# Half a key tile as VectorE's last softmax work, and turned denominators for the second last unit

## The chip, the core and the metric

The kernel runs on one core of a Trainium2 chip. The metric is the device time of one execution in microseconds. Five engines work from queues of their own: TensorE (PE in the profile; its weight loads are PEld), VectorE (DVE), ScalarE (ACT), GpSimd (POOL) and SyncE (SP); the last two, and ScalarE, also issue DMAs. Each engine takes its instructions in the order in which they were written, and an instruction that has to wait holds up those behind it on its engine.

## The reference

A gate mixes attention and a feed-forward block over the same input x (2048 x 512, bf16). There are 32 heads of 16 columns each.

```python
qkv = (x @ wqkv)...                              # q, k, v: 32 heads of 2048 x 16
scores = jnp.einsum("bhqd,bhkd->bhqk", q, k) * (Dh ** -0.5)
p = softmax(scores, axis=-1)
o = jnp.einsum("bhqk,bhkd->bhqd", p, v)
a = o.transpose(...).reshape(B, S, D) @ wo
b = (silu(x @ w_gate) * (x @ w_up)) @ w_down
g = sigmoid((x * gate_w).sum(-1, keepdims=True))
out = g * a + (1 - g) * b
```

## The kernel before

**Units and key tiles.** The queries form 4 blocks of 512 and the heads 8 groups of 4. One block of queries with one group of heads is a unit (`UNIT`, L115), so there are 32 units, 0 to 31. A unit has 16 key tiles of 128 keys. A key tile has four score blocks, one for each head, of 128 keys by 512 queries. TensorE computes a score block, an engine takes its exponential, and TensorE multiplies the result with v and adds it up over the unit's 16 key tiles in the accumulator `o_ps` (`pv`, L882). v has a column of ones, so that the softmax denominators come out as rows 0, 32, 64 and 96 of the accumulator, beside 16 rows of output for each head.

**Two engines share the exponentials.** ScalarE takes two score blocks at a time (`emit_pair`, L731): TensorE writes a tile `s_t` of 128x1024 in PSUM, of which there are two buffers, and one ACTIVATE makes `e_t` of it. VectorE takes whole key tiles from the end of a unit (`emit_d`, L764): each of the four score blocks comes in a PSUM bank of its own (`d_t`, three banks shared with all other small work, `m_tile`) and is scaled and converted to an integer in `y_t`, which is an approximate exponential by its bits. Then come five wide steps over the 128x2048 of the key tile that correct it: z is masked out of y, u is a linear function of z, u is squared, u is multiplied by z, u is added to y, and a last step (`last`, called its close below) shifts and scales y. The add is mostly a DMA that accumulates, issued from GpSimd; for the last work of unit 31 it is an instruction of VectorE (`here_add`, L791).

**The order.** The program keeps a plan of the times of TensorE, VectorE and ScalarE with costs written in the code, and places each instruction by it, before anything runs. `v_unit` (L1386) decides whether VectorE takes a further key tile: only if its work queued so far and a lead (`LEAD` 16.0 us, and `LAST` 8.5 us for unit 31) end before ScalarE would reach that tile. `next_pv` and the loops behind L1419 put the products with v, the feed-forward block and the projections into the time that TensorE has left beside the scores.

**The end of a unit.** The accumulator is evicted to `osb` (`post`). For most units the denominators go through DRAM to be inverted. The last two units take no such way. For unit 30 (`last_recip`, L1251) one matmul with `sbc_t` copies each denominator to the 32 rows of its head in PSUM (`dl`, 128x512), and VectorE inverts this in four quarters of 128x128, each followed by its product with `osb`. For unit 31 the code behind the loops (from L1500) does otherwise: four small matmuls with the columns of `osb` as weights and `sel_t` as the moving operand put the denominators into a tile of 128x16 (`dt`), with queries on the partitions; VectorE inverts these 16 columns (`rt`); sixteen matmuls with the identity as the moving operand turn and spread them again over 128x512 (`rps`); and the product with `osb` follows. The output projection of the last block of queries adds up in `a_l_a`, `a_l_b`, `al` and `al_o`.

Of the kernel before, what the change touches and what calls it, by code (L numbers as in the profile page):

```python
# [9 lines left out]
ALU = mybir.AluOpType  # L10
AX = mybir.AxisListType
BF16 = mybir.dt.bfloat16
F32 = mybir.dt.float32
U16 = mybir.dt.uint16
# [65 lines left out]
def kernel(  # L80
# [13 lines left out]
    P = 128  # L94
    x = A_x.flatten_outer_dims()
    S, D = x.shape
    F = B_w_gate.shape[1]
# [59 lines left out]
    def mm(*args, **kw):  # L157
        return ordered(nc.tensor.matmul(*args, **kw))  # L158
# [143 lines left out]
    def spend(mode, mms, ready=0.0):  # L302

        plan.seq += 1
        work_at.append((plan.pe, mms))
        plan.pe = max(plan.pe + (0.1 if mode != plan.mode else 0.0), ready) + (0.226 if mode == "F" else 0.216) * mms
        plan.mode = mode

    def later(cost, f, ready=None, key=None):

        c = plan.chain
        if c is not None:
            c.owed += 1
        ready = plan.pe + 0.25 if ready is None else ready
        owed.insert(sum(o[0] <= ready for o in owed), (ready, cost, f, c, key))
# [32 lines left out]
    def m_tile(name):  # L348
        while m_ready() is None:
            stuck()  # L350
        i = min((i for i in range(3) if banks[i] is not None), key=lambda i: banks[i])
        plan.pe = max(plan.pe, banks[i])
        banks[i] = None
        held[i] = ps_m[i].tile([P, QBW], F32, tag=f"m{i}", name=name)
        return held[i]

    def m_free(ps, t):
        i = [h is ps for h in held].index(True)
        banks[i], held[i] = t + 0.2, None
# [352 lines left out]
    pv_turn = [True]  # L712
    vready = []
    vcur = {}

    HEADS = (0, 2, 1, 3)

# [45 lines left out]

    def emit_d():  # L764
        if not vcur:
            vcur.update(n=v_take(), i=0, y=vex.tile([P, NV * QBW], U16, tag="y", name="y_t", bufs=NY))
            y_live[0] += 1
        n, i, y = vcur["n"], vcur["i"], vcur["y"]
        vcur["i"] += 1
        d_t = m_tile("d_t")  # L770
        score(d_t[:, :], 4 * n + i)
        spend("R", 1)
        e_of[4 * n + i] = y[:, i * QBW:(i + 1) * QBW].bitcast(BF16)
        if i == NV - 1:
            vcur.clear()

        def first():
            vec.tensor_scalar(out=y[:, i * QBW:(i + 1) * QBW], in0=d_t[:, :], scalar1=EXP_A, scalar2=EXP_B,
                              op0=ALU.mult, op1=ALU.add)
            m_free(d_t, plan.dve)  # L780
            if i < NV - 1:
                return
            z = vex.tile([P, NV * QBW], U16, tag="z", name="z_t")
            u_turn[0] ^= 1
            if u_turn[0]:

                ua = (kaug[:, 0, :] if au > QB else wd_t[:, 0:4, :].rearrange("p f d -> p (f d)")).bitcast(F16)
            else:
                ua = vex.tile([P, NV * QBW], F16, tag="u", name="u_t")[:, :]
            ya, za = y[:, :], z[:, :]  # L790
            here_add = n >= SLOTS - KT and act_end() - plan.dve < 4.2 + ADD_US  # L791
            key = ("y", n)
            plan.last = key
            vops.extend([
                (0.6, lambda: vec.tensor_scalar(out=za, in0=ya, scalar1=0x1FF, scalar2=0x800, op0=ALU.bitwise_and,
                                                 op1=ALU.bitwise_or), key, n),
                (0.6, lambda: vec.tensor_scalar(out=ua, in0=za, scalar1=EXP_K, scalar2=EXP_M, op0=ALU.mult,
                                                 op1=ALU.add), key, n),
                (1.135, lambda: vec.tensor_tensor(out=ua, in0=ua, in1=ua, op=ALU.mult), key, n),
            ])  # L800

            def add_here():
                vec.tensor_tensor(out=ya, in0=ya, in1=ua, op=ALU.add)
                added.append((plan.dve, last, n))

            def add():
                vec.tensor_tensor(out=ua, in0=ua, in1=za, op=ALU.mult)
                if here_add:
                    vops.append((1.135, add_here, None, n))
                    return  # L810
                nc.gpsimd.dma_start(out=ya, in_=ua, accum_op=ALU.add)  # L811
                added.append((plan.dve + ADD_US, last, n))

            def last():
                vec.tensor_scalar(out=ya, in0=ya, scalar1=EXP_D, scalar2=0.25, op0=ALU.add, op1=ALU.mult)
                vready.append((plan.dve + 0.4, n))
            vops.append((1.135, add, None, n))
        d_wait.append((plan.pe + 0.25, first, n))

    def pay_d():  # L820
# [119 lines left out]
    def recip16(o, i):  # L940
        with nc.allow_low_precision(reason="bf16 reciprocal of softmax denominators is plenty accurate here"):
            vec.reciprocal(o, i)
# [27 lines left out]
                normed.add((qb, b))  # L970
            at.setdefault(n0 + 13 + b, []).append(lambda norm=norm: later(0.345, norm))

    def recip_here(osb):

        dps = m_tile("dl")
        mm(dps[:, :], lhsT=sbc_t[:, :], rhs=osb[:, :], start=True, stop=True)
        rd = work.tile([P, QBW], BF16, tag="rd", name="rd")
        return dps, rd

    here_done = []  # L980
    a_ps = []
# [71 lines left out]
    def turn(dc, ps):  # L1053
        for k in range(2 * TQ):
            mm(ps[k // TQ][:, k % TQ * P:(k % TQ + 1) * P], lhsT=x_rows[:, k, (dc - HALF) * P:(dc - HALF + 1) * P],
               rhs=ident[:, :], start=True, stop=True)
# [179 lines left out]
    au = at_ = half = 0  # L1236
    vu = 0
    hi = [KT] * UNITS
    here = {}

    def finish(un):
        settle(un)
# [7 lines left out]

    def last_recip(un):  # L1251

        here[un] = recip_here(osbs[un])
        spend("F", 1)
        for i in range(TQ):
            def part(cs=slice(i * P, (i + 1) * P)):
                recip16(here[un][1][:, cs], here[un][0][:, cs])
                vec.tensor_tensor(out=osbs[un][:, cs], in0=osbs[un][:, cs], in1=here[un][1][:, cs],
                                  op=ALU.mult)
                if cs.stop == QBW:  # L1260
                    m_free(here[un][0], plan.dve)
                    here_done.append(un)
            later(1.2, part)

    def close(un):
        def f():
# [104 lines left out]
        emit_pv(ns[0])  # L1371

    SLACK = 0.1
    LEAD, LAST = 16.0, 8.5
    TILE_US = 1.87

    def forward():
# [3 lines left out]

    def act_end():
        left = [hi[u] - (at_ + half if u == au else 0) for u in range(au, UNITS)]
        return plan.act + sum(left) * TILE_US

    def v_unit():  # L1386

        nonlocal vu
        if y_live[0] >= NY or sum(v[0] for v in vops) > 1.4 or (au, at_) < (0, 2):
            return None  # L1390
        while vu < UNITS:
            if vu > au + 1 or vu in q_of and not (q_of[vu].done() and (vu < QB or plan.slot >= q_of[vu].done_at + 3)):
                return None
            left = hi[vu] - (at_ + half if vu == au else 0)
            if vu >= au and left > 0:
                end = plan.act + (left - 1) * TILE_US + ((hi[au] - at_) * TILE_US if vu > au else 0.0)
                if plan.dve + sum(v[0] for v in vops) + 0.6 * len(owed) + (LEAD if vu < UNITS - 1 else LAST) <= end:
                    return vu
            vu += 1
        return None  # L1400

    def v_take():
        un = v_unit()
        hi[un] -= 1
        n = un * KT + hi[un]
        forward()
        return n

    def want_d():
        if not vcur and v_unit() is None:  # L1410
            return False
        c = pick()
        one = c is not None and c.pieces[c.i][2] and (pace.credit > 0 or c.deadline <= plan.slot + 4)
        if len(d_wait) >= (1 if one else 2):
            return False
        t = m_ready(2 if one and int(c.pieces[c.i][2]) == 1 else 1)
        return t is not None and t <= plan.pe

    while au < UNITS:  # L1419
# [41 lines left out]
        n = au * KT + at_  # L1461
        emit_pair([4 * n + 2 * half, 4 * n + 2 * half + 1])
        half ^= 1
        at_ += not half
        forward()
    flush_act()
# [32 lines left out]
    osb = osbs[un]  # L1499
    tail(2)  # L1500
    dt = m_tile("dt")
    for tq in range(TQ):
        mm(dt[:, 4 * tq:4 * tq + 4], lhsT=osb[:, tq * P:(tq + 1) * P], rhs=sel_t[:, :], start=True, stop=True)
    rt = work.tile([P, 4 * TQ], BF16, tag="rt", name="rt")
    recip16(rt[:, :], dt[:, 0:4 * TQ])
    tail(2)
    rps = ps_s.tile([P, 2 * QBW], F32, tag="s", name="rps")
    for tq in range(TQ):
        for j in range(4):
            mm(rps[32 * j:32 * j + 32, tq * P:(tq + 1) * P],  # L1510
               lhsT=rt[:, 4 * tq + j:4 * tq + j + 1].broadcast_to([P, 32]), rhs=ident[:, :],
               start=True, stop=True, tile_position=(0, 32 * j), skip_group_check=True)
    tail(len(rest))
    on_l = work.tile([P, QBW], BF16, tag="rd", name="on_l")
    for tq in range(TQ):
# [46 lines left out]
```

## Time and profile before

| What | Value |
|---|---|
| Median of four runs | 828.84 us (826.58 to 829.12) |
| Profiled execution, time | 827.2 us |
| Profiled execution, span from the first to the last instruction | 825.5 us |
| Exponentials on ScalarE, e_t<-s_t | 842, 785.0 us busy |
| Score blocks on VectorE, y_t<-d_t | 364, 236.9 us busy |
| Granted clock of TensorE | 1.000 |

The chain that ended last, by the page, is a mixture of ScalarE and TensorE to which no single line contributes more than 6% of the span: the two hand on to each other all the time. Durations in the timelines are from start to end of an instruction; neighbours on one engine overlap a little, so the starts tell the pace. A line of a timeline with a count (x7) merges neighbours of one kind, and its duration goes from the first start to the last end. L158, L161 and L170 are the lines of helpers that record the instructions of TensorE, ScalarE and VectorE, so groups are told apart by their tiles.

### The profile page before, as it was taken

What the parts mean: (1) busy time and instruction counts of PE and PEld (TensorE: products, weight loads), DVE (VectorE), ACT (ScalarE), POOL (GpSimd) and SP (SyncE); (2) the same over time, 40 slices, a digit from 0 to 9 for tenths busy, and PEclk for the clock granted to TensorE, in tenths of its full rate; (3) what the DMA queues carried; (4) which work ended last, traced back from release to release, by engine and by line L of the source; (5) the groups of instructions that cost most, each with busy time, mean ns of one, the idle gap of its engine ahead of it and who ended that gap; (6) DMA issues with size and microseconds to landing.
All of it is one profiled execution on the core that took longest, in us unless ns stands there. A gap on an engine that the chain in (4) does not pass through costs nothing. (4 is left out here: it accounts for less than half of the span.)

```text
span 825.5 us, 20380 instructions
## 1 busy us (share of the span) xinstructions
PE 784.4 (95%) x8109; PEld 231.0 (28%) x8110; DVE 795.6 (96%) x1178; ACT 809.0 (98%) x911; POOL 105.8 (13%) x124
## 2 busy tenths in 40 slices
PE   8999999999999999899999999899999999899996
PEld 3322332322222222222222222222222222222222
DVE  6899999999999999999999999999999999999995
ACT  6999999999999999999999999999999999999996
POOL 5010111110111100101111111001111011111110
PEclk9999999999999999999999999999999999999999
DMA  7044346574543345465434455544344546534432
GB/s 179 12 77 91 57 89 124 123 160 97 109 93 74 77 97 126 93 126 101 84 72 94 104 126 115 112 78 100 74 93 88 117 103 120 106 62 88 85 82 58
DMA packets 101096, 79.75 MB, mean 97 GB/s; under 512 B 75745, under 2 KB 89033, under 8 KB 101001
## 3 DMA queue, kind: packets, MB, share of 16 engines
q0 software_dynamic: 12960, 47.19, 31.0%
q1 hardware_dynamic: 86312, 30.93, 15.8%
q8 instruction: 63, 1.03, 0.5%
q10 hardware_dynamic: 1728, 0.33, 0.2%
q14 instruction: 33, 0.26, 0.1%
HBM read 21.55 MB, written 2.35 MB: 29 GB/s over the span
## 5 line engine op out<-in xcount | busy, mean ns | idle before, releaser
L161 ACT ACTIVATE e_t<-s_t 128x1024 bf16<-128x1024 f32 x842 | 785.0, 1107 | 2.1 <-PE s_t L158 1.5
L158 PE MATMUL s_t<-qx,kaug 64*128 64x512 bf16 x1336 | 274.6, 383 | 25.7 <-ACT e_t L161 22.3
L170 DVE TENSOR_SCALAR y_t<-d_t 128x512 uint16<-128x512 f32 x364 | 236.9, 680 | 2.4 <-PE d_t L158 1.9
L158 PEld LDWEIGHTS <-kaug 64*128 64x128 bf16 x2048 | 110.3, 93 | 338.5 <-issue 328.9
L158 PE MATMUL o_ps<-e_t,vaug 128*32 128x512 bf16 x1684 | 167.9, 390 | 0.0
L158 PE MATMUL d_t<-qx,kaug 64*128 64x512 bf16 x296 | 100.2, 379 | 1.8 <-DVE y_t L170 0.5
L811 POOL DMA_DIRECT2D y_t<-u_t x45 | 46.6, 1036 | 356.1 <-PE s_t L158 228.6
L158 PEld LDWEIGHTS <-vaug 128*32 128x32 bf16 x2052 | 50.0, 93 | 121.4 <-issue 120.4
L811 POOL DMA_DIRECT2D y_t<-kaug x39 | 41.9, 1073 | 281.7 <-PE s_t L158 139.4
L158 PE MATMUL gu<-xT,wg 128*32 128x512 bf16 x896 | 76.1, 383 | 0.9 <-DMA wg<-in_B_w_gate_dram 0.6
L158 PE MATMUL gu<-xT,wu 128*32 128x512 bf16 x896 | 73.8, 382 | 0.0
L170 DVE TENSOR_SCALAR z_t<-y_t 128x2048 uint16<-128x2048 uint16 x91 | 62.4, 685 | 1.0
L170 DVE TENSOR_SCALAR y_t<-y_t 128x2048 uint16<-128x2048 uint16 x91 | 62.0, 683 | 1.3 <-DMA y_t<-u_t 0.8
L158 PE MATMUL ops<-wd_t,mt 128*32 128x512 bf16 x672 | 56.7, 383 | 0.0
L170 DVE TENSOR_TENSOR u_t<-u_t 128x2048 f16<-128x2048 f16 x45 | 54.8, 1218 | 0.8
L170 DVE TENSOR_TENSOR u_t<-u_t,z_t 128x2048 f16<-128x2048 f16 x45 | 54.6, 1214 | 0.1
L170 DVE TENSOR_TENSOR kaug<-kaug 128x2048 f16<-128x2048 f16 x40 | 48.8, 1221 | 1.0
L170 DVE TENSOR_TENSOR kaug<-kaug,z_t 128x2048 f16<-128x2048 f16 x40 | 48.5, 1214 | 0.1
L158 PE MATMUL s_t<-q,kaug 64*128 64x512 bf16 x208 | 42.3, 383 | 2.7 <-ACT e_t L161 2.4
L170 DVE SCALAR_TENSOR_TENSOR mt<-gs,gu 128x512 bf16<-128x512 bf16 x56 | 38.1, 680 | 2.5 <-PE gu L158 0.2
L170 DVE SCALAR_TENSOR_TENSOR gs<-th,gu 128x512 bf16<-128x512 bf16 x56 | 38.0, 679 | 0.3
L161 ACT ACTIVATE th<-gu 128x512 bf16<-128x512 f32 x56 | 37.7, 673 | 0.0
(147 smaller groups left out, 572.9 us busy)
## 6 DMA issues: line engine op xcount, KB each, us to landing
y_t<-u_t POOLq DMA_DIRECT2D x45, 512.0 KB, 5.1
y_t<-kaug POOLq DMA_DIRECT2D x39, 512.0 KB, 5.1
wg<-in_B_w_gate_dram SPq DMA_DIRECT2D x56, 128.0 KB
wu<-in_B_w_up_dram SPq DMA_DIRECT2D x56, 128.0 KB
y_t<-wd_t POOLq DMA_DIRECT2D x6, 512.0 KB, 5.0
on<-osb SPq DMA_DIRECT2D x120, 16.0 KB
rb<-rr SPq DMA_DIRECT2D x15, 128.0 KB
wd_t<-in_B_w_down_dram SPq DMA_DIRECT2D x7, 256.0 KB
```

Source lines behind the costliest of these rows:

```text
L158: return ordered(nc.tensor.matmul(*args, **kw))
L161: ordered(nc.scalar.activation(*args, **kw))
L170: return lambda *a, **kw: ordered(f(*a, **kw))
L811: nc.gpsimd.dma_start(out=ya, in_=ua, accum_op=ALU.add)
```

## The change

Three things are changed.

1. When no whole key tile can be given to VectorE any more, `v_half` may give it two of the four score blocks of one key tile of unit 31, once. ScalarE takes the first two blocks of that tile, as one pair, and VectorE the last two; all its steps are then 1024 columns wide in place of 2048 (`cols`), the add is done on VectorE, and the tile's product with v waits for both halves.
2. The denominators of unit 30 are inverted as those of unit 31: four small matmuls (`denominators`), a reciprocal of 128x16, sixteen matmuls (`spread_rows`) into the same bank, and one product of 128x512. The four steps are placed as two chains of side work, the second released after the first.
3. The lead `LAST` is 10.5 us in place of 8.5, with 6.0 us for the half tile (`LAST_HALF`), and the limit under which the add is done on VectorE is 6.2 us and the add's 6.0 in place of 4.2 and 6.0.

The tail behind the loops is the same code, with its two groups of matmuls moved into the new functions.

```diff
     def emit_d():
         if not vcur:
-            vcur.update(n=v_take(), i=0, y=vex.tile([P, NV * QBW], U16, tag="y", name="y_t", bufs=NY))
+            n, i = v_take()
+            vcur.update(n=n, i=i, y=vex.tile([P, NV * QBW], U16, tag="y", name="y_t", bufs=NY))
...
+        cols = slice(2 * QBW if n in halved else 0, NV * QBW)
+        part = (NV * QBW - cols.start) / (NV * QBW)
...
-            ya, za = y[:, :], z[:, :]
-            here_add = n >= SLOTS - KT and act_end() - plan.dve < 4.2 + ADD_US
+            ya, za, ua = y[:, cols], z[:, cols], ua[:, cols]
+            full, wide = 0.07 + 0.53 * part, 0.07 + 1.065 * part
+            here_add = n >= SLOTS - KT and (n in halved or act_end() - plan.dve < 6.2 + ADD_US)
...
             def last():
                 vec.tensor_scalar(out=ya, in0=ya, scalar1=EXP_D, scalar2=0.25, op0=ALU.add, op1=ALU.mult)
+                if n in halved:
+                    for k in (2, 3):
+                        e_end[4 * n + k] = plan.dve + 0.4
+                    return
                 vready.append((plan.dve + 0.4, n))
...
-    def recip_here(osb):
-
-        dps = m_tile("dl")
-        mm(dps[:, :], lhsT=sbc_t[:, :], rhs=osb[:, :], start=True, stop=True)
-        rd = work.tile([P, QBW], BF16, tag="rd", name="rd")
-        return dps, rd
+    def denominators(p, osb):
+        for tq in range(TQ):
+            mm(p[:, 4 * tq:4 * tq + 4], lhsT=osb[:, tq * P:(tq + 1) * P], rhs=sel_t[:, :], start=True, stop=True)
+
+    def spread_rows(p, rt):
+        for tq in range(TQ):
+            for j in range(4):
+                mm(p[32 * j:32 * j + 32, tq * P:(tq + 1) * P],
+                   lhsT=rt[:, 4 * tq + j:4 * tq + j + 1].broadcast_to([P, 32]), rhs=ident[:, :],
+                   start=True, stop=True, tile_position=(0, 32 * j), skip_group_check=True)
...
     def last_recip(un):
 
-        here[un] = recip_here(osbs[un])
-        spend("F", 1)
-        for i in range(TQ):
-            def part(cs=slice(i * P, (i + 1) * P)):
-                recip16(here[un][1][:, cs], here[un][0][:, cs])
-                vec.tensor_tensor(out=osbs[un][:, cs], in0=osbs[un][:, cs], in1=here[un][1][:, cs],
-                                  op=ALU.mult)
-                if cs.stop == QBW:
-                    m_free(here[un][0], plan.dve)
-                    here_done.append(un)
-            later(1.2, part)
+        st = {}
+        osb = osbs[un]
+
+        def turn():
+            st["p"] = m_tile("dl")
+            denominators(st["p"], osb)
+            spend("F", 1)
+            later(0.3, invert)
+
+        def invert():
+            st["r"] = work.tile([P, 4 * TQ], BF16, tag="rt", name="rt")
+            recip16(st["r"][:, :], st["p"][:, 0:4 * TQ])
+
+        def spread():
+            spread_rows(st["p"], st["r"])
+            spend("F", 2)
+            later(0.67, norm)
+
+        def norm():
+            vec.tensor_tensor(out=osb[:, :], in0=osb[:, :], in1=st["p"][:, :], op=ALU.mult)
+            m_free(st["p"], plan.dve)
+            here_done.append(un)
+        c = pace.add([(1, turn, True, "F", None)], 0, plan.slot + 2)
+        pace.add([(2, spread, False, "F", None)], 0, plan.slot + 4, [c], 1)
...
-    LEAD, LAST = 16.0, 8.5
+    LEAD, LAST, LAST_HALF = 16.0, 10.5, 6.0
...
+    def v_half():
+
+        un = UNITS - 1
+        if halved or au < un or y_live[0] >= NY or hi[un] - at_ < 3:
+            return False
+        busy = sum(v[0] for v in vops) + 0.6 * (len(owed) + len(d_wait) + len(added))
+        return plan.dve + busy + LAST > act_end() and plan.dve + busy + LAST_HALF <= act_end() - 0.5 * TILE_US
+
     def v_take():
         un = v_unit()
+        if un is None:
+            halved.append((UNITS - 1) * KT + hi[UNITS - 1] - 1)
+            return halved[0], 2
...
     def want_d():
-        if not vcur and v_unit() is None:
+        if not vcur and v_unit() is None and not v_half():
             return False
```

More of the change, by code (lines that the diff above doesn't have):

```diff
@@ L714 @@
     vcur = {}
+    halved = []
     HEADS = (0, 2, 1, 3)
@@ L794, in first @@
             vops.extend([
-                (0.6, lambda: vec.tensor_scalar(out=za, in0=ya, scalar1=0x1FF, scalar2=0x800, op0=ALU.bitwise_and,
+                (full, lambda: vec.tensor_scalar(out=za, in0=ya, scalar1=0x1FF, scalar2=0x800, op0=ALU.bitwise_and,
                                                  op1=ALU.bitwise_or), key, n),
-                (0.6, lambda: vec.tensor_scalar(out=ua, in0=za, scalar1=EXP_K, scalar2=EXP_M, op0=ALU.mult,
+                (full, lambda: vec.tensor_scalar(out=ua, in0=za, scalar1=EXP_K, scalar2=EXP_M, op0=ALU.mult,
                                                  op1=ALU.add), key, n),
-                (1.135, lambda: vec.tensor_tensor(out=ua, in0=ua, in1=ua, op=ALU.mult), key, n),
+                (wide, lambda: vec.tensor_tensor(out=ua, in0=ua, in1=ua, op=ALU.mult), key, n),
             ])
@@ L808, in add @@
                 if here_add:
-                    vops.append((1.135, add_here, None, n))
+                    vops.append((wide, add_here, None, n))
                     return
@@ L815, in last @@
                 vec.tensor_scalar(out=ya, in0=ya, scalar1=EXP_D, scalar2=0.25, op0=ALU.add, op1=ALU.mult)
+                if n in halved:
+                    for k in (2, 3):
+                        e_end[4 * n + k] = plan.dve + 0.4
+                    return
                 vready.append((plan.dve + 0.4, n))
-            vops.append((1.135, add, None, n))
+            vops.append((wide, add, None, n))
         d_wait.append((plan.pe + 0.25, first, n))
@@ L1238 @@
     hi = [KT] * UNITS
-    here = {}
     def finish(un):
@@ L1383, in act_end @@
         left = [hi[u] - (at_ + half if u == au else 0) for u in range(au, UNITS)]
-        return plan.act + sum(left) * TILE_US
+        return plan.act + (sum(left) - 0.5 * len(halved)) * TILE_US
     def v_unit():
         nonlocal vu
-        if y_live[0] >= NY or sum(v[0] for v in vops) > 1.4 or (au, at_) < (0, 2):
+        if halved or y_live[0] >= NY or sum(v[0] for v in vops) > 1.4 or (au, at_) < (0, 2):
             return None
@@ L1406, in v_take @@
         forward()
-        return n
+        return n, 0
     def want_d():
-        if not vcur and v_unit() is None:
+        if not vcur and v_unit() is None and not v_half():
             return False
@@ L1463 @@
         half ^= 1
+        if n in halved:
+            half = 0
         at_ += not half
@@ L1501 @@
     dt = m_tile("dt")
-    for tq in range(TQ):
-        mm(dt[:, 4 * tq:4 * tq + 4], lhsT=osb[:, tq * P:(tq + 1) * P], rhs=sel_t[:, :], start=True, stop=True)
+    denominators(dt, osb)
     rt = work.tile([P, 4 * TQ], BF16, tag="rt", name="rt")
@@ L1507 @@
     rps = ps_s.tile([P, 2 * QBW], F32, tag="s", name="rps")
[L1508 to L1512, printed above, removed]
+    spread_rows(rps, rt)
     tail(len(rest))
```

## The prediction

> **What bounds the kernel now.** I began with the page's totals. ScalarE is busy in 98% of the span and VectorE in 96%, so nothing can be gained by moving work between them except where one of them stops early, and that is at the end.
>
> ```profile
> span 825.5 us, 20380 instructions
> PE 784.4 (95%) x8109; PEld 231.0 (28%) x8110; DVE 795.6 (96%) x1178; ACT 809.0 (98%) x911; POOL 105.8 (13%) x124
> ```
>
> Next I set the instruction order of the two built programs side by side. It differs from the point where unit 30 (the second last) is normalised; all before that point is the same on every engine. On SP and POOL the order is the same to the end: no DMA is added, dropped or moved past another, the output store of o_t alone comes with its later VectorE instruction. The whole effect must therefore arise after about 797 us, and the timeline of the last 30 us is the view that decides. ScalarE first (start, duration, engine, operation, idle before):
>
> ```profile
> 810.12 6.63 ACT L161 ACTIVATE e_t<-s_t 128x1024 bf16<-128x1024 f32 x7
> 817.58 0.60 ACT L161 ACTIVATE osb<-o_ps 128x512 bf16<-128x512 f32 x1 [0.83 <-PE o_ps L158]
> ```
>
> The seven exponentials end at 816.75 and the last one takes about 1.2 (longer than the group mean of 1.107 on the page), so six starts fill 6.63 - 1.2 = 5.43 us: one exponential every 0.904 us, back to back. The eviction of the last unit (osb) starts 0.83 after them. Now VectorE over the same stretch:
>
> ```profile
> 797.15 0.69 DVE L170 TENSOR_SCALAR u_t<-z_t 128x2048 f16<-128x2048 uint16 x1
> 797.76 0.95 DVE L170 RECIPROCAL rd<-dl 128x128 bf16<-128x128 f32 x1
> 798.74 0.23 DVE L170 TENSOR_TENSOR osb<-osb,rd 128x128 bf16<-128x128 bf16 x1
> 798.89 0.95 DVE L170 RECIPROCAL rd<-dl 128x128 bf16<-128x128 f32 x1
> ...
> 802.27 1.22 DVE L170 TENSOR_TENSOR u_t<-u_t 128x2048 f16<-128x2048 f16 x1
> 803.40 1.28 DVE L170 TENSOR_SCALAR y_t<-d_t 128x512 uint16<-128x512 f32 x2
> ...
> 809.70 1.23 DVE L170 TENSOR_TENSOR kaug<-kaug 128x2048 f16<-128x2048 f16 x1
> 810.97 1.23 DVE L170 TENSOR_TENSOR kaug<-kaug,z_t 128x2048 f16<-128x2048 f16 x1
> 812.22 1.22 DVE L170 TENSOR_TENSOR y_t<-y_t,kaug 128x2048 uint16<-128x2048 uint16 x1
> 813.68 1.30 DVE L170 TENSOR_SCALAR y_t<-y_t 128x2048 uint16<-128x2048 uint16 x2 [0.23 <-DMA y_t<-u_t]
> 818.52 0.26 DVE L170 RECIPROCAL rt<-dt 128x16 bf16<-128x16 f32 x1 [3.54 <-PE dt L158]
> ```
>
> VectorE stops at 814.98 and stands idle for 3.54 us, while ScalarE works until 816.75: this is the slack that can be used. The starts also give a rule for the sums below: an instruction that needs the one before starts 0.04 after its end (798.74 after 797.76 + 0.95), one that doesn't starts 0.08 before it (798.89 after 798.74 + 0.23). TensorE last:
>
> ```profile
> 815.29 0.40 PE L158 MATMUL o_ps<-e_t,vaug 128*32 128x512 bf16 x4
> 815.52 0.39 PE L158 MATMUL o_ps<-y_t,vaug 128*32 128x512 bf16 x4
> 815.84 0.39 PE L158 MATMUL a_l_a<-bblk,ident 64*128 64x512 bf16 x1
> ...
> 816.16 0.82 PE L158 MATMUL al<-wo_t,on 128*128 128x512 bf16 x2
> 816.91 0.40 PE L158 MATMUL o_ps<-y_t,vaug 128*32 128x512 bf16 x4
> 817.14 0.39 PE L158 MATMUL o_ps<-e_t,vaug 128*32 128x512 bf16 x4
> ```
>
> None of these waits for anything: from 815.29 TensorE's own queue leads to the last o_ps at 817.14, 0.4 after the last exponential. So the end is set by ScalarE's pace and then by 1.85 us of queued matmuls. What follows (817.58 to 825.5, 7.92 us) is the same code in both kernels and stays.
>
> **Parts of the change.** *ScalarE.* Half a key tile, one pair of score blocks, goes to VectorE: 841 exponentials in place of 842. At 0.904 a start, the last one ends at 816.75 - 0.90 = 815.85, if it meets no more waits than now.
>
> *VectorE loses* the four reciprocals of 128x128 and their products: 797.76 to 802.27, 4.51 us. *It gains* one reciprocal of 128x16 (the same instruction is the last line above: 0.26), one product 128x512 with a PSUM operand, two evictions of scores (0.60 each by the pair at 803.40), and six half-wide steps. The product has no exact row. From below it is the group on<-on,rb (128x512, SBUF alone, 415 ns), from above the four quarters on_l<-osb,rps with the same kinds of operand (0.88 together); I take 0.68, the mean of the rows of this width that read PSUM. Half-wide steps (128x1024, 16 bit) have none either. TENSOR_SCALAR takes 285 ns at 512 columns (group aq<-qst) and 685 at 2048, so 0.42 in between; TENSOR_TENSOR 415 and about 1220, so 0.68. The bounds are those ends: three of each kind, 1.2 us earlier or 2.4 us later in all.
>
> A rule of the Trainium skill speaks against the half tile: "VectorE: DVE Perf Modes", section on the TRN2 errata, says that each instruction pays a fixed latency once, so that small tiles pay it more often. This case shows it too: the two TENSOR_SCALAR rows lie on a line with 0.15 us at no columns, so six half-steps carry about 0.9 us that buys nothing. By the page's formula (58 cycles and the columns over the mode's factor at 0.96 GHz) they would take an estimated 0.33 and 0.59, and the chain would end 0.54 earlier than by the rows, which changes nothing as TensorE ends last then.
>
> *The walk.* In the new order, from 797.15, with the rule above: square of u 797.88, small reciprocal 799.02, eviction 799.20, u times z 799.80, eviction 800.93, close of a finished unit 801.53 (its add was issued at 796.44 and landed 4.5 later, 800.9), product 802.13, third eviction 802.73. The fourth needs a matmul that stands on TensorE behind s_t and four o_ps (about 803.0 + 0.32 + 0.32, and 0.42 until it is read): 804.06, so VectorE is idle for some 0.73, which also covers either bound of the product. Then z 804.78, the half unit's two evictions 805.38 and 805.98, u 806.58, close of the other unit 807.19 (its add is issued about 801.5 and lands by 807.0 at the 5.5 us that it takes now), o_t 807.79, square 808.45, product with z 809.71, the half unit's z 810.86, u 811.32, square 811.78, product 812.50, add of the full unit 813.10 and its close 814.36, add of the half 814.97 and its close 815.69, end 816.11. VectorE ends 1.13 later than now, still before 817.14.
>
> *TensorE loses* one 128x512 matmul and gains four of 4 columns and sixteen of 128, which the tail already has, as rows show: 0.11 (818.23 to the next at 818.34) and 0.34 (818.87 to 819.21). They lie in slots between score pairs, where the exponentials cover them. "TensorE: Matmul & The Clock Gate", section LDWEIGHTS, would price the four small ones higher: columns over 1.2 in ns for a weight load, an estimated 0.43 for four. The row has four loads of 128 columns in 0.16 us, and the row decides; 0.43 would use up one slot's slack and cost some 0.2.
>
> *The waits added.* The small reciprocal waits for the four matmuls, and the product for the sixteen; both are done by then. Behind them stand evictions, and the matmuls of the next scores wait for those, because ops and dl hold two of three banks. The third score matmul cannot start before the second eviction ends, 801.53 + 0.68 = 802.21, and the score pair behind it then starts at 802.31, 0.49 before its exponential (799.59 to 800.08 in the records), which was due at 802.69: a stall of 0.1. Before loses as much between 799 and 801 us, so I charge nothing.
>
> *The end.* With the second last exponential over at 814.92 TensorE takes o_ps from 814.98, al 815.30, o_ps of the full unit 816.05, the last o_ps 816.27. ScalarE would allow 815.90, VectorE 816.17. So TensorE, against 817.14 now: 0.87 us less. Span 825.5 - 0.9 = 824.6. The profiled run took 827.2, 1.7 around its span, and lies 1.64 under the median of 828.84, whose four runs spread from 826.58 to 829.12; on the median I forecast 828.84 - 0.9 = **827.9**.
>
> **Rivals.** *The gain is hidden* (828.8). ScalarE has no slack, so each score pair that comes late is paid in full; the bank wait above is the place, and 0.3 at three such pairs eats it all. For it: two banks for six evictions. Against: the walk finds one stall of 0.1.
>
> *The half unit sets the end, slower.* VectorE's last close decides once it ends after 817.08, 0.97 later than the walk. At the upper bound (half steps as dear as full ones) it ends at 818.52 and the last o_ps moves from 817.14 to 818.58: 830.3. For it: ten steps in a row without cover. Against: the 512-column rows, less than half of the 2048 ones.
>
> *The half tile is not taken* or helps nothing, and only the reciprocals go: VectorE idles 3 us longer at the end, and the time stays at 828.8. The built order shows half-wide rows and one exponential fewer, which speaks against it.
>
> **Numbers.** Forecast 0.53; hidden 0.22; slower rival 0.20; not taken or anything else 0.05. The forecast's own range of gains, 0.4 to 1.1, is 827.7 to 828.4 on the median. The whole range goes from 825.7 (0.9 under the lowest run, if more runs fall there) to 829.7 (most of the slower rival). 0.3%, 2.5 us, is about what a measurement of this kernel can tell from no change; a loss of that size needs the upper bound of the slower rival and further waits, a gain of that size a median made of runs like the lowest: faster 0.09, same 0.86, slower 0.05.
>
> **What would show it.** Right: 841 exponentials, the last ending near 815.9; the close of the half unit ending near 816.1; the last o_ps at 816.2 to 816.4 with no wait of note; half steps of 0.42 and 0.68. Wrong: gaps over 0.2 between exponentials from 800 to 806 (hidden), or the last o_ps waiting for VectorE after 817 (slower).

## The result, and the profile after

| | Before | After |
|---|---|---|
| Median | 828.21 us (63 runs, 826.58 to 830.83) | 827.51 us (42 runs, 826.15 to 830.39) |
| Ratio to before, 95% interval | | 0.999 (0.9985 to 0.9995) |
| Span of the profiled execution | 825.5 us | 825.6 us |
| Exponentials on ScalarE | 842 | 841 |

The change takes 0.7 us off, 0.4 to 1.2 by the interval. The two spans of the profiled executions do not show it, and here is how to see why. The program is the same up to the normalisation of unit 30, and yet that point comes later in the second record. In the timeline of VectorE the last CAST to osb is the eviction of unit 30. It is shown first for the kernel before, and then for the changed kernel with the rest of what the prediction speaks of (start, duration, engine, operation, idle before):

```profile
795.83 0.68 DVE L170 CAST osb<-o_ps 128x512 bf16<-128x512 f32 x1
```

```profile
796.78 0.68 DVE L170 CAST osb<-o_ps 128x512 bf16<-128x512 f32 x1
...
805.07 0.69 DVE L170 TENSOR_SCALAR y_t<-d_t 128x512 uint16<-128x512 f32 x1 [0.58 <-PE d_t L158]
...
811.97 0.43 DVE L170 TENSOR_SCALAR z_t<-y_t 128x1024 uint16<-128x1024 uint16 x1
...
812.89 0.69 DVE L170 TENSOR_TENSOR u_t<-u_t 128x1024 f16<-128x1024 f16 x1
...
816.81 0.43 DVE L170 TENSOR_SCALAR y_t<-y_t 128x1024 uint16<-128x1024 uint16 x1
818.66 0.26 DVE L170 RECIPROCAL rt<-dt 128x16 bf16<-128x16 f32 x1 [1.43 <-PE dt L158]
```

So 0.95 us of difference between two executions of the same instructions lies ahead of the change. From that eviction on, before takes 825.5 - 795.83 = 29.67 us and after 825.6 - 796.78 = 28.82: 0.85 less. The idle time of VectorE before the last reciprocal falls from 3.54 to 1.43. The end of ScalarE's and of TensorE's work in the changed kernel:

```profile
794.49 22.27 ACT L161 ACTIVATE e_t<-s_t 128x1024 bf16<-128x1024 f32 x24
817.72 0.60 ACT L161 ACTIVATE osb<-o_ps 128x512 bf16<-128x512 f32 x1 [0.95 <-PE o_ps L158]
```

```profile
815.90 0.39 PE L158 MATMUL o_ps<-e_t,vaug 128*32 128x512 bf16 x2 [0.20 <-ACT e_t L161]
816.23 0.82 PE L158 MATMUL al<-wo_t,on 128*128 128x512 bf16 x2
816.98 0.40 PE L158 MATMUL o_ps<-y_t,vaug 128*32 128x512 bf16 x4
817.21 0.38 PE L158 MATMUL o_ps<-e_t,vaug 128*32 128x512 bf16 x2
817.29 0.39 PE L158 MATMUL o_ps<-y_t,vaug 128*32 128x512 bf16 x2
```

The last exponential ends at 816.76. TensorE's queue brings the last products to 817.21, and the two that need VectorE's half start at 817.29, 0.05 after its close ended at 816.81 + 0.43 = 817.24. All three engines now end within 0.6 us of one another.

### The profile page after: what moved, and what is told of

The parts are those of the page before. It is cut to its first block, busy times and chain, and to the rows that moved or that the text cites. A ratio compares the mean times of both kernels' runs of the same rounds, so it can differ in the third digit from the quotient of the medians.

```text
span 825.6 us, 20410 instructions
## 1 busy us (share of the span) xinstructions
PE 784.6 (95%) x8124; PEld 230.7 (28%) x8125; DVE 796.6 (96%) x1180; ACT 809.0 (98%) x910; POOL 106.0 (13%) x124
## 5 line engine op out<-in xcount | busy, mean ns | idle before, releaser
L170 DVE TENSOR_TENSOR u_t<-u_t 128x2048 f16<-128x2048 f16 (+1 forms) x46 | 55.5, 1207 | 0.9
L170 DVE TENSOR_TENSOR u_t<-u_t,z_t 128x2048 f16<-128x2048 f16 (+1 forms) x46 | 55.3, 1202 | 0.2
```

What stands on the lines that cost most here:

```text
L170: return lambda *a, **kw: ordered(f(*a, **kw))
```

## The experiments

Much of what separates two executions lies ahead of the change: over the 14 records below the eviction of unit 30 starts anywhere from 795.18 to 797.97 us, though VectorE and ScalarE have the same order of instructions up to there. So the experiments are read in one stretch of their records: from the start of unit 30's eviction (the CAST above) to the start of the last o_ps matmuls. Beside it stand the end of ScalarE's last exponential, counted from the same start, and what follows the stretch to the end of the span. A changed kernel without a ratio was run once, for its record.

| Kernel | Stretch, us | Last exponential ends, us | Rest, us | Ratio to before (interval) |
|---|---|---|---|---|
| before, first and second record | 21.31, 22.12 | 20.92, 20.91 | 8.4, 8.3 | |
| closes swapped, wide reciprocals | 21.16 | 20.98 | 8.4 | 1.0003 (0.9994 to 1.0012) |
| turned denominators alone, two records | 21.04, 21.08 | 20.94, 20.98 | 8.3, 8.3 | 0.9987 (0.9978 to 0.9996), 0.9999 (0.9989 to 1.0010) |
| the change, two records | 20.51, 20.58 | 19.98, 20.06 | 8.3, 8.3 | 0.999 (0.9985 to 0.9995) |
| and one al matmul moved back | 20.57 | 20.05 | 8.3 | |
| and no steps for the half tile | 20.43 | 19.98 | 8.3 | |
| both of these | 20.30 | 20.06 | 8.3 | |
| the change, store scaled late | 20.44 | 19.99 | 8.3 | 0.9983 (0.9971 to 0.9996) |
| and one al matmul moved back | 20.27 | 20.04 | 8.3 | 0.9982 (0.9969 to 0.9994) |
| half tile with wide reciprocals | 23.25 | 19.98 | 10.4 | 1.0045 (1.0028 to 1.0062) |
| a whole further tile | 23.64 | 19.11 | 9.1 | 1.0040 (1.0025 to 1.0055) |

The third column separates two things. With 842 exponentials ScalarE ends 20.91 to 20.98 us after the eviction in every record, whichever way unit 30 is normalised; with 841 it ends at 19.98 to 20.06. So the half tile takes 0.9 us off ScalarE's end each time. What lies between ScalarE's end and the last o_ps is the part that the other engines set: 0.39 and 1.21 before, 0.18 with the closes swapped, 0.10 with the turned denominators alone, 0.53 and 0.52 with the change.

### The same kernels again

> The kernel before again, for the spread of the measure between executions. From the start of unit 30's eviction to the start of the last o_ps: 21.31 us if the stretch repeats; theory: within 0.1 of it, whatever the whole time is. Rival: the stretch itself varies by 0.5 or more between executions, and the difference of 0.80 between the first two records says little.

> The changed kernel again: theory 20.51 us within 0.1; rival: it varies by 0.5 or more.

The changed kernel repeats (20.58 against 20.51). Before does not: 22.12 against 21.31, as the rival has it, so the 0.80 between the first two records lies within what before itself varies by. Its second record shows the place, on VectorE and then on TensorE:

```profile
815.98 1.29 DVE L170 TENSOR_SCALAR y_t<-y_t 128x2048 uint16<-128x2048 uint16 x2 [1.53 <-DMA y_t<-u_t]
```

```profile
817.33 0.40 PE L158 MATMUL o_ps<-y_t,vaug 128*32 128x512 bf16 x4 [0.63 <-DVE y_t L170]
...
818.96 0.39 PE L158 MATMUL o_ps<-e_t,vaug 128*32 128x512 bf16 x4
```

VectorE waits 1.53 us for an add by DMA, where the first record had 0.23, and the close of unit 31's last tile, which stands behind it in the queue, is late too. TensorE then waits 0.63 with everything that follows. ScalarE's end is where it was (20.91); the whole loss comes behind it. The add landed 6.7 us after its issue here and 5.5 in the first record. In the changed kernel the same add is issued earlier, 5.6 us after unit 30's eviction in place of 12.4, because u is multiplied before the normalisation rather than after it; it landed after 4.7 and 4.9 us, and nobody waits for it.

### The normalisation alone

```diff
     def v_half():
-        if halved or au < un or y_live[0] >= NY or hi[un] - at_ < 3:
+        if True:
             return False
```

> The turned denominators alone; no half tile, so ScalarE keeps 842 exponentials. Measure: from the start of unit 30's eviction on VectorE (the last CAST to osb) to the start of the last o_ps matmuls; 21.31 us before (795.83 to 817.14), 20.51 with the whole change (796.78 to 817.29). Theory (the normalisation only frees VectorE, and VectorE is not what ends last): 21.2 to 21.4, VectorE's last close some 5 us ahead of it, time 828.2, ratio 1.000. Rival (the cheaper normalisation is itself worth the gain): 20.5, time 827.5, ratio 0.999.

> The turned denominators alone again, on the chip of the run above: theory 21.5 us in the same measure (21.48 before), ratio to before within 0.9980 to 0.9995; the whole change had 20.94 and 21.01, so that the half tile is worth some 0.5 by the records. Rival: the stretch differs by 0.5 from the first record, and nothing can be told of the half tile's share.

21.04 and 21.08: under the 21.2 to 21.4 that I expected, and far from the rival's 20.5. The times do not repeat that verdict. The first ratio, 0.9987, was the rival's and not the 1.000 expected; the second, 0.9999, lies outside the range expected for it. The eviction in the first record, and then its end, on ScalarE and TensorE:

```profile
795.54 0.68 DVE L170 CAST osb<-o_ps 128x512 bf16<-128x512 f32 x1
```

```profile
799.78 16.70 ACT L161 ACTIVATE e_t<-s_t 128x1024 bf16<-128x1024 f32 x18
```

```profile
815.62 0.81 PE L158 MATMUL al<-wo_t,on 128*128 128x512 bf16 x2 [0.53 <-ACT e_t L161]
816.35 0.61 PE L158 MATMUL o_ps<-e_t,vaug 128*32 128x512 bf16 x8
```

VectorE is out of the way (its last close ended at 811.65), so both of its o_ps groups have moved ahead, and TensorE now does wait: al needs a PSUM buffer that ScalarE gives back. The exponentials end at 816.48 and the last o_ps group starts 0.10 later, at 816.58. That is ScalarE's limit: with 842 exponentials hardly more than this 0.10 can be won here. The half tile then shortens the stretch by 0.5 us (21.06 to 20.55 between the means of the two records each). One exponential fewer frees 0.9 on ScalarE, and 0.4 of it is lost again, because VectorE's products with v stand behind the last score pair in TensorE's queue once more (0.10 grows to 0.52). What the turned denominators are worth by themselves stays open: 0.25 against the first record of before, 1.06 against the second. The two timings, 0.9987 and 0.9999 on different chips, do not tell 0.25 us from nothing.

### The closes swapped, nothing else

```diff
             def add_here():
                 vec.tensor_tensor(out=ya, in0=ya, in1=ua, op=ALU.add)
-                added.append((plan.dve, last, n))
+                added.insert(0, (plan.dve, last, n))
```

> The kernel before with one thing changed: on VectorE the close of the last key tile, whose add VectorE does itself, comes ahead of the close that waits for the add by DMA, and its product with v goes one score pair earlier on TensorE. Nothing is left out, the wide reciprocals stay. Theory (the gain of the turned denominators alone came from an add by DMA that no longer lands late, and from one o_ps group fewer in TensorE's queue after the last score pair): from unit 30's eviction on VectorE to the eviction of unit 31 on ScalarE 21.5 us, as with the turned denominators alone (21.48), against 21.75 and 22.56 in the two records of before; time some 0.3 to 0.8 under before, ratio 0.9990 to 0.9996. Rival (the four wide reciprocals were themselves on the path): 21.75 or more, ratio 1.000.

One line each of VectorE, TensorE and ScalarE:

```profile
797.97 0.68 DVE L170 CAST osb<-o_ps 128x512 bf16<-128x512 f32 x1
...
819.13 0.39 PE L158 MATMUL o_ps<-e_t,vaug 128*32 128x512 bf16 x4
...
819.57 0.60 ACT L161 ACTIVATE osb<-o_ps 128x512 bf16<-128x512 f32 x1 [0.61 <-PE o_ps L158]
```

From the eviction of unit 30 to that of unit 31 it is 819.57 - 797.97 = 21.60 us, as expected within 0.1. That is 0.12 from the turned denominators (21.48) and only 0.15 from the better record of before (21.75), in a single record. ScalarE's end tells more: it comes at 20.98 here, no later with wide reciprocals than with turned ones, and the part behind it shrinks from 0.39 to 0.18, about the 0.23 that one o_ps group takes on TensorE. So where the add by DMA is not late, the four reciprocals were not themselves on the path. In the second record of before they were, by a detour: they stand ahead of the step that issues the add and so delay it, and the add landed too late. The time shows no gain (1.0003, and 0.9990 to 0.9996 was expected): I cannot claim from it how much the late adds cost on average.

### The half tile without the cheap normalisation, and a whole tile

The first restores the four wide reciprocals, and sets `LAST_HALF` to 3.0. The second is the changed kernel with

```diff
-        if halved or au < un or y_live[0] >= NY or hi[un] - at_ < 3:
+        if True:
...
-    LEAD, LAST, LAST_HALF = 16.0, 10.5, 6.0
+    LEAD, LAST, LAST_HALF = 16.0, 8.5, 6.0
```

and 4.2 in place of 6.2 in `here_add`.

> The half tile alone, with the four wide reciprocals of before (the lead for the half tile is lowered from 6.0 to 3.0, without which it is not taken). 841 exponentials. Theory (VectorE then ends last): walking its new order at the durations of the records its last close ends 818.84 in the times of before, so the last o_ps starts 23.1 us after unit 30's eviction in place of 21.31, and the time is 1.8 us longer than before: 830.0, ratio 1.002. Rival (the number of exponentials alone sets the end): 20.4, 0.9 shorter than before, 827.3.

> Turned denominators with the old leads (8.5 and 4.2) and no half tile: VectorE then takes a whole further key tile of unit 31, ScalarE has 840 exponentials, two fewer than before. Theory (VectorE ends last): its walk ends 819.24 in the times of before, last o_ps 23.5 us after unit 30's eviction in place of 21.31, time 2.2 longer than before: 830.4, ratio 1.0026. Rival (ScalarE's count sets the end): 19.5, 1.8 shorter, 826.4.

Both are slower, as expected of a VectorE that ends last, and the stretches agree with the walks (23.25 for 23.1, 23.64 for 23.5). The times are longer than expected by 1.1 and 0.6 us. The rest of the span, which was taken to stay at 8.3, grew to 10.4 and 9.1 and more than covers this. TensorE in the first of the two:

```profile
818.75 0.62 PE L158 MATMUL o_ps<-y_t,vaug 128*32 128x512 bf16 x4 [2.37 <-DVE y_t L170]
819.12 0.66 PE L158 MATMUL o_ps<-e_t,vaug 128*32 128x512 bf16 x2
819.15 0.64 PE L158 MATMUL o_ps<-y_t,vaug 128*32 128x512 bf16 x2
819.73 0.61 PE L158 MATMUL al<-wo_l,osb 128*128 128x512 bf16 x1
```

and busy time in windows of the same kernel (the window's length, then PE, PEld, DVE, ACT and POOL, then the granted clock, DMA share and GB/s):

```profile
816.00:818.00 2.00, 0.38 (x1) 0.09 (x1) 2.00 (x3) 0.00 (x0) 0.00 (x0) 1.00 0.00 0
818.00:819.00 1.00, 0.25 (x4) 0.14 (x6) 1.00 (x3) 0.00 (x0) 0.00 (x0) 0.55 0.00 0
819.00:820.00 1.00, 1.00 (x9) 0.23 (x3) 0.03 (x1) 0.16 (x1) 0.00 (x0) 0.50 0.00 0
...
823.00:824.00 1.00, 1.00 (x4) 0.42 (x3) 0.27 (x2) 0.00 (x0) 0.00 (x0) 0.50 0.00 0
```

After the wait of 2.37 us TensorE is at half its clock, and the same matmuls that take 0.38 elsewhere take 0.61 to 0.66, all but the last of them. In the second kernel the wait is longer:

```profile
819.72 1.22 PE L158 MATMUL o_ps<-y_t,vaug 128*32 128x512 bf16 x8 [2.73 <-DVE y_t L170]
```

### Which limit holds the changed kernel

In the first kernel the half tile's z, u, square, product and add are left out (`n in halved or vec...`, five times). In the second, one al matmul goes behind the last o_ps groups (the edit below). The third does both.

```diff
-            tail(3)
+            tail(2)
...
     osb = osbs[un]
-    tail(2)
+    tail(3)
     dt = m_tile("dt")
```

> The whole change, but the half tile gets no correction (z, u, square, product and add of the half unit are left out; evictions and close stay, with the program order otherwise the same). VectorE ends 3.0 us earlier. Theory (VectorE and TensorE's queue tie in the changed kernel, 817.29 against 817.21): the last o_ps starts 20.43 us after unit 30's eviction, only 0.08 less than 20.51. Rival (VectorE alone sets the end): it falls to what ScalarE allows, 816.83, so 20.05.

> The changed kernel with one of the three al matmuls moved from ahead of the last two o_ps groups to behind them (0.22 us of TensorE's queue). Theory (VectorE's last close, 817.24, holds the last group anyway): 20.5 us from unit 30's eviction to the start of the last o_ps, nothing gained. Rival (TensorE's queue sets the end): 20.3.

> Both at once: the half tile without its correction steps (left out: z, u, square, product, add) and one al matmul moved behind. Theory (two limits that tie; only both together move the end): 20.2 us, 0.3 less than the changed kernel, near what ScalarE allows (816.83, 20.05). Rival (one of the two sets the end alone): the same as the better of the two single runs.

20.43, 20.57 and 20.30: two limits that nearly tie. Taking 3 us from VectorE gives 0.08 or 0.15 (against the two records of the change; 0.08 against the one in which ScalarE ends at 19.98 too). Taking 0.22 from TensorE's queue gives nothing; the record shows the last two products waiting for VectorE's half instead:

```profile
817.37 0.40 PE L158 MATMUL o_ps<-y_t,vaug 128*32 128x512 bf16 x4
817.59 0.38 PE L158 MATMUL o_ps<-e_t,vaug 128*32 128x512 bf16 x2
817.89 0.40 PE L158 MATMUL o_ps<-y_t,vaug 128*32 128x512 bf16 x2
```

Only both together give the 0.2 to 0.3.

### The same with nothing left out

```diff
+    put_off = []
...
-                       lambda k: wo_t[:, k, :] if k < NB else wd_t[:, k - NB, :], lambda p: later(0.65, lambda: end(p)))
+                       lambda k: wo_t[:, k, :] if k < NB else wd_t[:, k - NB, :],
+                       lambda p: put_off.append(lambda: end(p)) if (qb, tq) == (QB - 2, TQ - 1) else later(0.65, lambda: end(p)))
...
         next_pv()
+    for f in put_off:
+        f()
```

> The changed kernel with the last scaling of a finished output tile (o_t from ops, 0.66 us of VectorE) placed behind the close of the half unit instead of in the middle of its chain; nothing is left out. VectorE's close ends some 0.66 earlier (816.58 in the times of the changed kernel's record). Theory (tie with TensorE's queue): the last o_ps starts 20.43 us after unit 30's eviction in place of 20.51; time 827.4, ratio to before 0.999. Rival (VectorE alone sets the end): 20.05, 0.46 less.

> Both that and one al matmul moved behind the last o_ps groups. Theory: TensorE's queue is 0.22 shorter there and VectorE no longer holds it: 20.2 us, 0.3 less than the changed kernel; time 827.2, ratio to before 0.9988. Rival (the matmul moved back is paid after the eviction of unit 31, so that nothing is won to the end of the span): last o_ps at 20.2, but the rest grows from 8.3 to 8.6 and the time is 827.5.

The scaling of the last finished output tile needs no place in VectorE's chain; behind the close it frees 0.66 us. Alone it brings 20.44, with the al matmul 20.27. The rest stays at 8.3, and by the record the rival of the second run falls, though the median of its times, 827.51, is the rival's. The end of the second on TensorE:

```profile
815.22 0.40 PE L158 MATMUL o_ps<-y_t,vaug 128*32 128x512 bf16 x4
815.44 0.38 PE L158 MATMUL o_ps<-e_t,vaug 128*32 128x512 bf16 x2
815.45 0.38 PE L158 MATMUL o_ps<-y_t,vaug 128*32 128x512 bf16 x2
```

By the records this version is some 0.3 us shorter than the change, and its interval (0.9969 to 0.9994) lies wholly under before. That it beats the changed kernel the timings do not show; the intervals overlap.

## Why the prediction was right

*The number.* Forecast were 0.9 us and a median of 827.9; measured were 0.7 us and 827.51. The median lies under the forecast's own range of 827.7 to 828.4, and within the whole range of 825.7 to 829.7. The base did that: the four runs of before had a median of 828.84, 63 runs have 828.21, and 0.9 off this is 827.3. The gain lies in the forecast's range of 0.4 to 1.1. The whole range would have held a change of nothing as well, so the marks of the mechanism weigh more than the time.

*ScalarE.* One exponential fewer, ending at 815.85 in the times of before: measured 816.76 - 0.95 = 815.81. Right, and the records with 842 and 841 exponentials confirm it: ScalarE's end moves by 0.9 with the half tile and not with the normalisation.

*VectorE.* The walk ended at 816.11; measured 817.24 - 0.95 = 816.29. The half-wide steps took 0.43 and 0.69 for my 0.42 and 0.68, and the product of 128x512 took the 0.68 that I gave it. The idle time ahead of the fourth eviction was 0.58 for 0.73. One slip remains: the half tile's z started 1.26 after the wide product instead of 1.15, with the gap of an instruction that needs the one before.

*TensorE.* The last o_ps at 816.27; measured 817.21 - 0.95 = 816.26 for the part that ScalarE feeds and 816.34 for VectorE's. I named TensorE's queue as the limit, with VectorE 0.1 under it. It is VectorE by 0.08, and the five kernels on this show a tie, so naming either was a matter of a tenth.

*The bank wait.* I expected a stall of 0.1 at the score pair behind the third score matmul. There is none: the matmul went at 802.88, after the eviction had ended at 802.69, and ScalarE kept its pace. The working had a slip here. It takes 801.53 for the start of the second eviction, but in the walk that is the start of the close behind it; the eviction starts at 800.93. With this it ends at 801.61 and no stall follows (measured, 802.69 - 0.95 = 801.74). The pairs that were late are others, as in before. The slip cost nothing, as the stall was not charged.

*The slower rival* was real as a mechanism: both kernels in which VectorE ends last are slower by 2 to 5 us. Part of that is the fallen clock. The rival did not come true here because the close ended at 816.29 in the times of before, 0.8 ahead of the 817.08 from which the change would lose, and my upper bound for the half steps was far off, as the nearest rows said.

*What the prediction took for granted* is that before's tail is a constant. It took the 0.23 us of waiting for the add by DMA as part of the base, and valued the normalisation alone at nothing. The second record has 1.53 there, and the first record of the normalisation alone is 0.27 shorter than even the better one of before. The sum of 0.87 is right for the two first records (0.80 in the stretch, 0.85 to the end of the span). By the experiments some 0.25 of it comes with the turned denominators, through the o_ps groups that moved ahead, and 0.5 with the half tile. Against the second record of before the change is worth 1.6 us. That the record the prediction was read from had the short wait is luck, and how often the long one comes no run here shows.

## What to carry to other kernels

When two executions differ by more than the change is worth, measure from a point where both programs are still the same, and compare that stretch. Within that stretch, note where the bounding engine ends and what comes behind it: the two answer to different changes. Where several engines are brought to end together, a further gain needs work taken from all that tie; one alone gave 0.08 at most here, and the al matmul nothing. A small wait for a DMA in one record is a warning, not a constant: look whether a reordering can issue that DMA earlier.

## What the hardware showed that was not expected

TensorE lost half its clock in a short wait. It stood idle for 2.37 us in one kernel and 2.73 in another. The granted clock was 1.00 before and 0.50 afterwards: from 818.1 to 824.9 in the first, where the fall came 1.7 us after the last matmul had ended, and from 819.5 to 822.9 in the second. "TensorE: Matmul & The Clock Gate" of the Trainium skill, Part 1, explains such a drop by a window of activity of about 3.4 us. The waits here are shorter than that, and the clock fell all the same; but the low clock lasted 3.4 us in the second kernel and twice that, 6.8, in the first, which fits the length that the page gives. In the kernels where TensorE waited no longer than 0.63 us in this stretch it kept 1.00 through its last matmul.

The same add by DMA of 512 KB landed 4.7 to 4.9 us after its issue where that came 5.6 us after unit 30's eviction, and 5.4 to 6.7 after it where it came about 12.4 us after, where the store of an output tile from SP's queue lies within its flight each time. Whether the store delays it was not tried.
